# Attention and a routed expert layer in one kernel: four small moves in the order of the expert stage

## The chip, the cores and the metric

The kernel runs as one program on one core of a Trainium2 chip. The metric is device time in microseconds (us). The engines are named as in the profile: PE (TensorE), DVE (VectorE), ACT (ScalarE), POOL (GpSimd) and SP (SyncE, which issues most of the transfers). Each engine takes its instructions in the order in which the program emits them, and waits for others on semaphores.

## The reference

Inputs are `q`, `k`, `v` of 4 batches, 8 heads, 768 positions and 64 channels, a gate and the two weight matrices of each of 8 experts. First comes an attention with a window and block summaries, then a routed expert layer on its rows:

```python
mask_l = np.abs(pos[:, None] - pos[None, :]) < 16
scores_l = scale * np.matmul(q, k.transpose(0, 1, 3, 2))          # inside the window
scores_s = scale * einsum(q, k.reshape(..., 32, D).max(3)) + log(32)  # 24 block summaries
a = softmax(concat([where(mask_l, scores_l, -1e9), scores_s]))
x = a @ concat([v, block means of v])          # (4, 768, 512) after joining the heads
for each row s of a batch:
    e = argmax(x[s] @ w_gate) if local_gate(x[s]) < 0.5 or s == 0 else previous e
    h = np.maximum(x[s] @ w1[e], 0.0)           # 512 -> 1024
    out[s] = softmax(x[s] @ w_gate)[e] * (h @ w2[e])   # 1024 -> 512
```

## The kernel before

**Attention and routing.** The first third of the program is the attention, in 48 groups. Its rows go to DRAM as `x_dram`. VectorE works out each row's expert and its place in lists of rows sorted by expert (`route`, `early`, `finish`). Rows of one expert are cut into blocks of 128.

**The expert stage.** Weights are held as two parts, `hi` (rounded to a short format by an ACT cast, L1119) and `lo` (the difference, by a subtraction on DVE at L1122 or, in four pieces, on POOL at L1127). Each product is therefore three matmuls (hi by hi, hi by lo, lo by hi). `split` makes both parts of one chunk of 1024 columns; a matrix has four chunks. `SPLIT_BY` says by letters who subtracts each chunk: "VGVV" for the first matrix (chunk 1 on POOL, the others on DVE), "VVVV" for a second matrix after the first call. Raw weights come into two staging tiles `stg` by DMA from SP (`refill`, L1442), two halves of 1 MB for each matrix.

**Calls.** Blocks are served three, two or one at a time, and which calls run is decided on the chip: values are loaded into registers, and skipped calls are branched over (`tc.If`, lines 1604, 1608, 1618, 1623). With these inputs run, in order: three early pairs, `call3(0)`, `few(0)`, `call3(1)`, `few(1)`, `call3(2)` to `call3(4)`, `call2(0)`, and `call1(0)`. `few` serves up to 32 rows of an expert with unsplit weights. The experts change (new weights are split) at `call3(3)`, `call2(0)` and `call1(0)`.

**One call.** `blocks` runs the first layer (L1213 to L1215) into three rotating PSUM banks `s0`, `s1`, `s1` (printed as `bs`), each group ended by a relu on ACT (L1219) and a subtraction on DVE (L1221); then the second layer (L1165 to L1167) block by block into banks `a2` and `a` (printed `ba`). The sums of the second block are left in bank `a` ("kept"); the first block's second layer and the scaling of the kept sums are done by `left_over` at the head of the next call, where the next first-layer weights are split beside them (`hook`, `w1`). `store` scales sums into `yo` on ACT or DVE and sends them out by an indirect DMA from POOL (L1178). Second-layer weights are split by `own` beside the first layer. `late` fetches the next expert's weights into `stg` once the old ones have been read; `refill` ties such a fetch to a given matmul by a manual dependency. `single` (L1251) serves one block: its first layer goes in two runs of 12 products (`mm1(0)`, `mm1(1)`), between them four transposes (`th`), then the second layer.

**The planner.** Routing work of the last batch is woven between the matmuls of the first calls. Its steps are generators that yield a kind ("DVE", "LONG", "LONGER", "PE", ...). `flow(C_T)` is called after each short run of matmuls, moves the planner's clock on by 0.65 and emits every step that is ready by it; a DVE step adds its cost to the planner's DVE time `q` (0.1, or `C_LONG`), and a "PE" step is emitted only when the clock has reached its ready time. The four "LONGER" steps at L1051 and L1057 lead to the "PE" step of L1083, 24 matmuls that bring each slot's gate weights, and the index and scale columns of the few rows, into slot order.

**Lines touched.** `C_LONG` (L73), `left_over` (L1191), the first layer and the fetches in `blocks` (L1201), the bank of `few` (L1323), `splits` (L1457), `call2` (L1545), and the `left_over` ahead of `call1(0)` (L1619).

Of the kernel before, what the change touches and what calls it, by code (L numbers as in the profile page):

```python
# [32 lines left out]
KT, FT = DM // P, DF // P  # L33
# [8 lines left out]
AT1 = AT2 + 2 + 2 * (N2 + MORE)  # L42
SLOTS = AT1 + 2 + N1 + MORE
LANE1, LANE2 = N3 + MORE, N3 + MORE + 1
LANE3 = LANE2 + N2 + MORE
# [24 lines left out]
ON_PE = {"PE": 2, "PE late": 3}  # L70

C_T, C_PE, C_WAIT, C_DVE, C_LAT, AHEAD = 0.65, 0.8, 0.3, 0.1, 0.1, 1.5
C_LONG = {"LONG": 0.9, "LONGER": 1.7}  # L73

LOCAL_THR = -1.4e-7

# [1 line left out]
class Kernel:  # L78
# [1111 lines left out]

    def left_over(self, i, w1=None):  # L1191

        self.store(self.kept, i + 1, True)

        def hook(f):
            if w1 and f < 4:
                w1(f)

        self.store((yield from self.second_layer(0, hook)), i, True)

    def blocks(self, i, k, mid, w1=None, w2=None, between=None, refill=None, own=None):  # L1201

        nc = self.nc
        n, per = k * P, 2 if k == 2 else 1
        xT, hT = self.xT, self.hT
        xh, xl = [[xT[:, c, part, 0:k].rearrange("p h t -> p (h t)") for c in range(KT)] for part in range(2)]
        for f in range(0, FT, per):
            ps = self.bank("s")[:, 0:per * n].rearrange("p (f t) -> p f t", f=per)
            for j in range(per):
                for c in range(KT):  # L1210
                    c0 = self.w1_at(f + j, c)
                    wh, wl = [w[0][:, c0:c0 + P] for w in (self.hi, self.lo)]
                    nc.tensor.matmul(out=ps[:, j], lhsT=wh, rhs=xh[c], start=(c == 0), stop=False)  # L1213
                    nc.tensor.matmul(out=ps[:, j], lhsT=wh, rhs=xl[c], start=False, stop=False)  # L1214
                    ins = nc.tensor.matmul(out=ps[:, j], lhsT=wl, rhs=xh[c], start=False, stop=(c == KT - 1)).ins  # L1215
                    if k > 2 or c % 2:
                        yield
            h, l = hT[:, f:f + per, 0, 0:n], hT[:, f:f + per, 1, 0:n]
            nc.scalar.activation(out=h, in_=ps, func=AF.Relu)  # L1219
            self.dve(0.6, self.t + 0.5)  # L1220
            nc.vector.scalar_tensor_tensor(out=l, in0=ps, scalar=0.0, in1=h.bitcast(F32), op0=ALU.max, op1=ALU.subtract)  # L1221
            if refill and f == 0:
                refill(0, ins)
            if own and f < 4:
                own(*range(f, f + per))
            if refill and f == 4:
                refill(1, ins)
        early = w2 is not None
        halves = range(k) if early else range(k - 1, 0, -1)
        pm, last = PM0 if i == 0 else PM2 if not early and k == 2 else PM, FT * (len(halves) - 1)  # L1230
        for half in halves:

            def hook(f):
                j = FT * abs(half - halves[0]) + f
                if i > EARLY and j == pm[0]:
                    nc.gpsimd.drain()
                if j in pm:
                    mid(pm.index(j))
                if between and j == last + 4:
                    between()  # L1240
                for at, w in (PW1, w1), ([last + x for x in PW2], w2):
                    if w and j in at:
                        w(*(q for q in range(4) if at[q] == j))

            kept = not early and half == halves[-1]
            yp = yield from self.second_layer(half, hook, kept)
            if not kept:
                self.store(yp, i + half, i < EARLY or half == k - 1)
        yield
# [55 lines left out]
    def few(self, j):  # L1305


        nc, fw, xT = self.nc, self.fw, self.few_xT
        w1, w2 = self.few_w
        h = fw.tile([P, 2, P], F32, name="few_h")  # L1310
        hT = fw.tile([P, 2, 4, FEW], F32, name="few_hT")
        hp = [self.bank("s") for c in range(2)]
        for c in range(2):
            for k in range(KT):
                for q in range(4):
                    o = self.w1_at(2 * q + c, k)
                    nc.tensor.matmul(out=hp[c][32 * q:32 * q + 32, 0:P], lhsT=xT[:, k], rhs=w1[:, o:o + P], start=(k == 0), stop=(k == KT - 1))
            nc.scalar.activation(out=h[:, c], in_=hp[c][:, 0:P], func=AF.Relu)
        for c in range(2):
            m = self.bank("t")  # L1320
            nc.tensor.transpose(out=m[:, 0:P], in_=h[:, c], identity=self.ident)
            nc.vector.tensor_copy(out=hT[:, c], in_=m[:, 0:P].rearrange("p (q t) -> p q t", q=4))
        yp = self.bank("a")  # L1323
        order = [*range(0, FT, 2), *range(1, FT, 2)]
        for f in order:
            for d in range(4):
                o = f * DM + P * d
                nc.tensor.matmul(out=yp[32 * d:32 * d + 32, 0:P], lhsT=hT[:, f % 2, f // 2], rhs=w2[:, o:o + P],
                                 start=(f == order[0]), stop=(f == order[-1]))
        y = fw.tile([P, P], F32, name="few_y")  # L1330
        nc.vector.tensor_scalar(out=y, in0=yp[:, 0:P], scalar1=self.psort4[:, j:j + 1], scalar2=None, op0=ALU.mult)  # L1331
        nc.gpsimd.indirect_dma_start(out=self.out.rearrange("t (q d) -> (t q) d", q=4),
                                     out_offset=bass.IndirectOffsetOnAxis(ap=self.sidx4[:, j:j + 1], axis=0),
                                     in_=y, in_offset=None, bounds_check=4 * T_ALL - 1, oob_is_err=False)

    def run(self):
        nc, tc = self.nc, self.tc
# [110 lines left out]
        def split(w, chunks, by=None):  # L1448
            for q in chunks:
                eng = nc.vector if SPLIT_BY[by or w][q] == "V" else nc.gpsimd  # L1450
                self.split(w, q * CH, q * CH + CH, st["stage"][w][:, q * CH:q * CH + CH], eng)
# [2 lines left out]
            while "words" not in st:  # L1454
                self.small(1, True)

        def splits(w, lane):  # L1457
            new = []

            def weights(*chunks):  # L1460
                if lane is None:
                    return
                if lane == LANE1:
                    split(w, chunks)
                    if chunks[-1] == NCH - 1:
                        st["spent"].append(w)
                        refills()
                    return
                if not new:
                    have_all()  # L1470
                    new.append(reg(lane, (ENG.Activation, ENG.DVE, ENG.Pool), 1))
                with tc.If(new[0] > 0):  # L1472
                    split(w, chunks, 2 if w and lane else None)

            return weights

        def late(lane):
            r = []

            def weights(w, after):  # L1480
                have_all()
                if not r:
                    r.extend((reg(2 * LANES + lane, (ENG.SP,), 1), reg(LANES + lane, (ENG.SP,), E - 1)))
                with tc.If(r[0] > 0):
                    refill(w, r[1], after)

            return weights

        def calls(n, blocks, lane):

            def mid(half):
                if half < blocks:
                    while n < AT2 and st["next"] <= n + half:
                        self.small(1, True)
                    self.tx(n + half, half)
                    if n < AT2:
                        freed()
                    elif n + half + blocks < (AT1, SLOTS)[n >= AT1]:
                        self.gather(n + half + blocks)

            return mid, splits(0, lane), splits(1, lane)
# [9 lines left out]
        with ExitStack() as ctx:  # L1511
# [33 lines left out]
            def call2(n):  # L1545
                i = AT2 + 2 + 2 * n
                yield from self.left_over(i - 2, splits(0, LANE2 + n))
                yield from self.blocks(i, 2, calls(i + 2, 2, None)[0], None, None, None, late(LANE2 + n), splits(1, LANE2 + n))

            def emit(*what):  # L1550
                for _ in chain(*what):
                    pass
# [63 lines left out]
                self.single(i, *calls(i + 1, 1, LANE3 + n + 1), late(LANE3 + n), own)  # L1616

            with tc.If(n1 > 0) as some:
                emit(self.left_over(AT1, splits(0, LANE3)))  # L1619
                call1(0)  # L1620
                with ExitStack() as c:
                    for n in range(1, N1):
                        c.enter_context(tc.If(n1 > CALL * n))
                        call1(n)
# [93 lines left out]
```

## Time and profile before

| | us |
|---|---|
| three runs | 442.80, 446.03, 447.43 (median 446.03) |
| profiled execution, its own time | 443.36 |
| its span in the trace | 441.6 |
| PE busy | 418.5 (95%) |
| DVE busy | 233.5 (53%) |
| ACT busy | 197.6 (45%) |
| POOL busy | 175.7 (40%) |
| stage fetches (1 MB each, 16 of them), issue to landing, median | 7.8 |

The profile is of one execution. A timeline row gives the start, the length, the engine and line, what is written from what, shapes and count; in brackets, how long that engine sat idle before it and what ended the wait. Matmuls overlap, so their lengths are more than the time from one to the next. The granted TensorE clock is 1.00 of full speed (2.4 GHz) in almost all of the span.

### The profile page before, as it was taken

Reading aid. Unit: us, or ns where it says so; the run is one execution under the profiler, and the core shown is the slowest. Engines: PE = TensorE matmul, PEld = TensorE weight load, DVE = VectorE, ACT = ScalarE, POOL = GpSimd, SP = SyncE. Lnnn points to the kernel's source line nnn. Section 1 sums busy time; section 2 is a strip of 40 time slices with the busy share of each in tenths; the row PEclk is TensorE's granted clock in tenths of the full one; section 3 lists DMA queues with packets and bytes.
Section 4 is the critical chain, followed back from the end, with each engine's and each line's share of the span. In section 5 each row is a group of like instructions: output and inputs, shape, how many; then the busy total and the mean of one; then the engine's idle time right before and its main releaser. Section 6 shows DMA issues by size and latency. Waiting matters only on the chain. (4 is left out here: it accounts for less than half of the span.)

```text
span 441.6 us, 11260 instructions
## 1 busy us (share of the span) xinstructions
PE 418.5 (95%) x4228; PEld 360.7 (82%) x4228; DVE 233.5 (53%) x577; ACT 197.6 (45%) x466; POOL 175.7 (40%) x263
## 2 busy tenths in 40 slices
PE   8899989899999999999999999999999999999873
PEld 4678878678888797989987998799899899889652
DVE  5766687988775689957731122112174112247270
ACT  4968887787754217322121122122363212255451
POOL 3687585878524205845022103110350310361241
PEclk9989999999999999999999999999999999999998
DMA  8999989998260840393068802010347210309301
GB/s 315 402 364 393 388 301 357 380 406 338 71 227 19 322 197 12 98 390 123 1 242 308 345 26 77 21 49 0 95 156 276 96 49 0 94 33 382 108 24 55
DMA packets 22277, 83.24 MB, mean 189 GB/s; under 512 B 2702, under 2 KB 3344, under 8 KB 19120
## 3 DMA queue, kind: packets, MB, share of 16 engines
q1 hardware_dynamic: 17600, 67.74, 40.3%
q0 software_dynamic: 4448, 14.29, 9.4%
q8 instruction: 39, 0.64, 0.6%
q14 instruction: 46, 0.38, 0.3%
q10 hardware_dynamic: 144, 0.20, 0.1%
HBM read 69.63 MB, written 12.71 MB: 186 GB/s over the span
## 5 line engine op out<-in xcount | busy, mean ns | idle before, releaser
L1213 PE MATMUL bs<-xT,h 128*128 128x384 f32 (+1 forms) x288 | 91.4, 317 | 0.0
L1214 PE MATMUL bs<-xT,h 128*128 128x384 f32 (+1 forms) x288 | 89.8, 312 | 0.0
L1215 PE MATMUL bs<-xT,l 128*128 128x384 f32 (+1 forms) x288 | 89.7, 311 | 0.0
L1165 PE MATMUL ba<-h,hT 128*128 128x512 f32 x192 | 78.6, 410 | 2.8 <-DVE few_y L1331 1.1
L1167 PE MATMUL ba<-h,hT 128*128 128x512 f32 x192 | 75.3, 392 | 0.8 <-DVE hT L1139 0.8
L1166 PE MATMUL ba<-l,hT 128*128 128x512 f32 x192 | 75.1, 391 | 0.0
L1221 DVE SCALAR_TENSOR_TENSOR hT<-bs,hT 128x384 fp32r<-128x384 f32 (+1 forms) x56 | 33.2, 593 | 75.6 <-ACT hT L1219 61.8
L1133 POOL DMA_INDIRECT xg<-x_dram,gidx x30 | 29.7, 990 | 102.4 <-PE bt L1144 88.0
L1219 ACT ACTIVATE hT<-bs 128x384 fp32r<-128x384 f32 (+1 forms) x56 | 29.3, 523 | 85.3 <-PE bs L1215 83.4
L1213 PEld LDWEIGHTS bs<-xT,h 128*128 128x128 f32 x288 | 54.5, 189 | 0.9 <-issue 0.4
L1214 PEld LDWEIGHTS bs<-xT,h 128*128 128x128 f32 x288 | 54.5, 189 | 0.4
L1215 PEld LDWEIGHTS bs<-xT,l 128*128 128x128 f32 x288 | 54.5, 189 | 0.0
L319 ACT ACTIVATE pr<-bs,nm 128x120 f32<-128x120 f32 x192 | 51.0, 355 | 6.1 <-DVE nm L311 4.7
L1178 POOL DMA_INDIRECT out_dram<-yo,sidx x24 | 26.5, 1103 | 59.5 <-ACT yo L1174 36.1
L1122 DVE TENSOR_TENSOR l<-stg,h 128x1024 fp32r<-128x1024 f32 x26 | 35.2, 1378 | 25.1 <-ACT h L1119 24.9
L1165 PEld LDWEIGHTS ba<-h,hT 128*128 128x128 f32 x192 | 36.1, 188 | 10.6 <-issue 2.7
L1167 PEld LDWEIGHTS ba<-h,hT 128*128 128x128 f32 x192 | 36.1, 188 | 9.3 <-DVE hT L1139 1.3
L1174 ACT ACTIVATE yo<-ba,psort 128x512 f32<-128x512 f32 x24 | 16.5, 686 | 56.2 <-PE ba L1167 43.2
L1166 PEld LDWEIGHTS ba<-l,hT 128*128 128x128 f32 x192 | 36.2, 189 | 6.1
L1139 DVE TENSOR_TENSOR xT<-bt,xT 128x512 fp32r<-128x512 f32 x27 | 18.6, 691 | 40.9 <-ACT xT L1137 35.9
L1127 POOL TENSOR_TENSOR l<-stg,h 128x256 fp32r<-128x256 f32 x24 | 29.8, 1271 | 16.8 <-ACT h L1119 16.7
L1119 ACT CAST h<-stg 128x1024 fp32r<-128x1024 f32 x32 | 32.1, 1045 | 4.0 <-PE ba L1167 2.5
(265 smaller groups left out, 652.6 us busy)
## 6 DMA issues: line engine op xcount, KB each, us to landing
stg<-in_w SPq DMA_DIRECT2D x16, 1024.0 KB, 7.8
vw<-in_vW SPq DMA_DIRECT2D x16, 780.0 KB, 7.3
few_w<-in_w SPq DMA_DIRECT2D x8, 1024.0 KB, 8.5
kp<-in_kT SPq DMA_DIRECT2D x16, 384.0 KB, 6.2
q<-in_qT SPq DMA_DIRECT2D x16, 384.0 KB, 6.8
vt<-in_vT SPq DMA_DIRECT2D x16, 384.0 KB, 6.5
x_dram<-xs SPq DMA_DIRECT2D x8, 768.0 KB, 5.5
wst<-in_w SPq DMA_DIRECT2D x8, 512.0 KB, 6.8
```

Source lines behind the costliest of these rows:

```text
L319: nc.scalar.activation(out=pr[:, h, u, 0:W], in_=sp[:, h, u, :], func=AF.Exp, bias=nm[:, h, u:u + 1], scale=1.0)
L1119: self.nc.scalar.copy(out=hi, in_=src)
L1122: eng.tensor_tensor(out=lo, in0=src, in1=hi.bitcast(F32), op=ALU.subtract)
L1127: eng.tensor_tensor(out=lo[:, p], in0=src[:, p], in1=hi[:, p].bitcast(F32), op=ALU.subtract)
L1133: self.nc.gpsimd.indirect_dma_start(out=t, out_offset=None, in_=rows, in_offset=bass.IndirectOffsetOnAxis(ap=self.gidx[:, i:i + 1], axis=0))
L1165: nc.tensor.matmul(out=ps, lhsT=ah, rhs=wh, start=first, stop=False)
L1166: nc.tensor.matmul(out=ps, lhsT=ah, rhs=wl, start=False, stop=False)
L1167: self.last_mm = nc.tensor.matmul(out=ps, lhsT=al, rhs=wh, start=False, stop=last).ins
L1213: nc.tensor.matmul(out=ps[:, j], lhsT=wh, rhs=xh[c], start=(c == 0), stop=False)
L1214: nc.tensor.matmul(out=ps[:, j], lhsT=wh, rhs=xl[c], start=False, stop=False)
L1215: ins = nc.tensor.matmul(out=ps[:, j], lhsT=wl, rhs=xh[c], start=False, stop=(c == KT - 1)).ins
L1221: nc.vector.scalar_tensor_tensor(out=l, in0=ps, scalar=0.0, in1=h.bitcast(F32), op0=ALU.max, op1=ALU.subtract)
```

## The change

Four things are edited. The planner's cost of a "LONGER" step goes from 1.7 to 1.85. `left_over` scales and sends the kept sums after the four hooks that split first-layer weights, and no more ahead of them. In `blocks`, both fetches are tied to the call's very first matmul, where each was tied to the last matmul of a group, and the second matrix's fetch is emitted in group 0 where the call does not split its own second-layer weights. `few` takes its sums' bank from the rotating first-layer banks, where it took `a2`. `call2` splits its second-layer weights all at once ahead of `blocks`, and the `left_over` ahead of `call1(0)` lets DVE subtract all four first-layer chunks.

```diff
-C_LONG = {"LONG": 0.9, "LONGER": 1.7}
+C_LONG = {"LONG": 0.9, "LONGER": 1.85}
...
     def left_over(self, i, w1=None):
 
-        self.store(self.kept, i + 1, True)
-
         def hook(f):
             if w1 and f < 4:
                 w1(f)
+            if f == 4:
+                self.store(self.kept, i + 1, True)
...
+        first = None
...
-                    nc.tensor.matmul(out=ps[:, j], lhsT=wh, rhs=xh[c], start=(c == 0), stop=False)
+                    ins = nc.tensor.matmul(out=ps[:, j], lhsT=wh, rhs=xh[c], start=(c == 0), stop=False).ins
+                    first = ins if f + j + c == 0 else first
...
             if refill and f == 0:
-                refill(0, ins)
+                refill(0, first)
             if own and f < 4:
-                own(*range(f, f + per))
-            if refill and f == 4:
-                refill(1, ins)
+                own(f)
+            if refill and f == (4 if own else 0):
+                refill(1, first)
...
-        yp = self.bank("a")
+        yp = self.bank("s")
...
-        def splits(w, lane):
+        def splits(w, lane, by=None):
...
-                    split(w, chunks, 2 if w and lane else None)
+                    split(w, chunks, by or (2 if w and lane else None))
...
                 yield from self.left_over(i - 2, splits(0, LANE2 + n))
-                yield from self.blocks(i, 2, calls(i + 2, 2, None)[0], None, None, None, late(LANE2 + n), splits(1, LANE2 + n))
+                splits(1, LANE2 + n)(0, 1, 2, 3)
+                yield from self.blocks(i, 2, calls(i + 2, 2, None)[0], None, None, None, late(LANE2 + n))
...
-                emit(self.left_over(AT1, splits(0, LANE3)))
+                emit(self.left_over(AT1, splits(0, LANE3, 2)))
```

## Rows read from the trace of the kernel before

**Rows 1.** Waits of PE, whole span: us in total, times, longest.
```profile
PE bs L1166 <- POOL l L1127: 1.7, 3, 0.7
...
PE ba L1165 <- DVE few_y L1331: 1.1, 2, 0.6
...
PE ba L1167 <- DVE hT L1139: 0.8, 1, 0.8
...
PE bt L1083 <- DVE bp L1078: 0.7, 1, 0.7
```

**Rows 2.** Busy time by stretch: PE, PEld, DVE, ACT, POOL, then granted clock, DMA.
```profile
387.40:411.20 23.80, 23.61 (x152) 21.24 (x152) 13.22 (x13) 12.60 (x16) 8.87 (x8) 1.00 0.59 220
411.20:434.00 22.80, 19.30 (x84) 14.16 (x84) 11.74 (x10) 11.79 (x15) 8.65 (x7) 1.00 0.11 40
```

**Rows 3.** Timeline of PE around the planner's product at L1083.
```profile
216.28 0.33 PE L1214 MATMUL bs<-xT,h 128*128 128x384 f32 x1
216.45 0.34 PE L1215 MATMUL bs<-xT,l 128*128 128x384 f32 x1
217.47 2.28 PE L1083 MATMUL bt<-bp,A 128*128 128x202 bf16 x24 [0.68 <-DVE bp L1078]
```

**Rows 4.** Timeline of all engines at the end of `few(1)`.
```profile
281.56 1.06 PE L1328 MATMUL ba<-few_w,few_hT 128*32 128x128 f32 x32
282.69 0.35 DVE L1331 TENSOR_SCALAR few_y<-ba,psort 128x128 f32<-128x128 f32 x1 [1.62 <-PE ba L1328]
283.19 0.47 PE L1165 MATMUL ba<-h,hT 128*128 128x512 f32 x1 [0.57 <-DVE few_y L1331]
```

**Rows 5.** Timeline of all engines, last `left_over` and `single`.
```profile
412.13 0.47 PE L1165 MATMUL ba<-h,hT 128*128 128x512 f32 x1 [1.03 <-PEq L1606]
...
413.69 0.69 ACT L1174 ACTIVATE yo<-ba,psort 128x512 f32<-128x512 f32 x1 [6.08 <-DMA xg<-x_dram,gidx]
...
415.42 3.89 ACT L1119 CAST h<-stg 128x1024 fp32r<-128x1024 f32 x4 [1.04 <-issue]
...
416.50 1.23 DVE L1122 TENSOR_TENSOR l<-stg,h 128x1024 fp32r<-128x1024 f32 x1 [8.17 <-ACT h L1119]
...
417.50 4.84 POOL L1127 TENSOR_TENSOR l<-stg,h 128x256 fp32r<-128x256 f32 x4 [1.46 <-ACT h L1119]
...
417.66 0.40 PE L1165 MATMUL bs<-h,xT 128*128 128x512 f32 x1
...
418.39 6.17 DVE L1122 TENSOR_TENSOR l<-stg,h 128x1024 fp32r<-128x1024 f32 x4 [0.67 <-ACT h L1119]
...
419.80 1.98 ACT L1119 CAST h<-stg 128x1024 fp32r<-128x1024 f32 x2
...
424.35 0.60 PE L1144 MATMUL bt<-ident,hs 128*128 128x128 f32 x4
...
424.73 2.36 DVE L1122 TENSOR_TENSOR l<-stg,h 128x1024 fp32r<-128x1024 f32 x2 [0.17 <-ACT h L1119]
...
427.01 0.69 DVE L1139 TENSOR_TENSOR hT<-bt,hT 128x512 fp32r<-128x512 f32 x1
...
427.75 0.50 PE L1167 MATMUL ba<-h,hT 128*128 128x512 f32 x1 [0.83 <-DVE hT L1139]
```

**Rows 6.** Timeline of all engines in the first layer of `call2(0)`.
```profile
393.32 0.69 ACT L1174 ACTIVATE yo<-ba,psort 128x512 f32<-128x512 f32 x1
396.11 0.60 ACT L1219 ACTIVATE hT<-bs 128x512 fp32r<-128x512 f32 x1 [2.10 <-PE bs L1215]
...
401.67 0.28 PE L1213 MATMUL bs<-xT,h 128*128 128x256 f32 x1
```

**Rows 7.** Line L1127 (POOL's subtractions): durations in ns, min, median, max.
```profile
L1127 POOL TENSOR_TENSOR l<-stg,h x24: 718/822/2433, 169.7 to 420.6; 128x256 fp32r<-128x256 f32 x24
```

**Rows 8.** Timeline of SP: the last fetch of second-layer weights.
```profile
402.03 1.66 SPq L1115 DMA_DIRECT2D stg<-in_w  x2
```

**Rows 9.** DMA issues: KB each, median us from issue to landing.
```profile
stg<-in_w SPq DMA_DIRECT2D x16, 1024.0 KB, 7.8
```

More of the change, by code (lines that the diff above doesn't have):

```diff
@@ L1212, in blocks @@
                     wh, wl = [w[0][:, c0:c0 + P] for w in (self.hi, self.lo)]
-                    nc.tensor.matmul(out=ps[:, j], lhsT=wh, rhs=xh[c], start=(c == 0), stop=False)
+                    ins = nc.tensor.matmul(out=ps[:, j], lhsT=wh, rhs=xh[c], start=(c == 0), stop=False).ins
+                    first = ins if f + j + c == 0 else first
                     nc.tensor.matmul(out=ps[:, j], lhsT=wh, rhs=xl[c], start=False, stop=False)
-                    ins = nc.tensor.matmul(out=ps[:, j], lhsT=wl, rhs=xh[c], start=False, stop=(c == KT - 1)).ins
+                    nc.tensor.matmul(out=ps[:, j], lhsT=wl, rhs=xh[c], start=False, stop=(c == KT - 1))
                     if k > 2 or c % 2:
```

## Prediction

> **What bounds the kernel now.** I read three views in this order: the waits of PE over the whole span, the busy time by stretch, and the timeline at the places that the edits touch. The waits say that PE is the bound and where it still loses time that an edit could touch: differences from POOL in `single`, the few rows' scaling, one late operand of the second layer, and DVE's columns for L1083 [rows 1]. The stretches say where there is anything to win. In 387.4 to 411.2 (`call2(0)`) PE is busy 23.61 of 23.80 us, so no edit there can gain more than 0.2 us; in 411.2 to 434.0 (`left_over` and `single`) it is busy 19.30 of 22.80, both at a granted clock of 1.00, the 2.4 GHz level [rows 2]. So the sum is about places where PE stands still, and each is priced from its own timeline. An edit that moves work of another engine is worth only what PE stops waiting for.
>
> **The planner's cost.** The last product before L1083 starts at 216.45, 0.17 us after its predecessor, and L1083 at 217.47 [rows 3]. Against that pace 1.02 - 0.17 = 0.85 us are lost. Four LONGER steps lead to it, so its ready time in the planner moves by at most 4 x 0.15 = 0.60. That is under one step of 0.65, so it is emitted one step later (chance 0.60 / 0.65, about 9 in 10) or not at all later. One step here is three products, 3 x 0.174 = 0.52 us of work that PE does inside the wait. DVE's columns come when they did, so L1083 and what follows (the index of the few rows, SP's fetch of their weights) start when they did, and nothing is pushed out. Gain 0.5; bounds 0 and 0.85.
>
> **The few rows' bank.** After `few`, the next second layer writes `a2`, which DVE still reads: PE idles 0.57 us and its first product takes 0.47 instead of 0.40 [rows 4]. This happens twice, 1.1 us of idle time [rows 1]. With the sums in a first-layer bank, the last reader of `a2` is the scaling of a block that was summed before the kept one, all of `few` and a second layer of 24 products earlier. The first-layer bank is free again long before the next first layer, a whole block's second layer (24 products) later. Gain 2 x 0.65 = 1.3; bounds 0 (another wait takes its place) and 1.7 (2 x 0.85, if the restart costs nothing).
>
> **Casts first, and no POOL, in the last call.** Now ACT first scales the kept sums at 413.69, and the four casts run from 415.42 at 3.89 / 4 = 0.97 us each, after 1.04 us in which ACT waits for nothing shown. POOL subtracts chunk 1 from 417.50 to 422.34, while `single` needs chunks 0 and 1 from 417.66 on. PE restarts at 412.13 and makes 24 products by 417.66, 0.23 us each; the 18 products of `single` ahead of its transposes would end at 417.66 + 18 x 0.23 = 421.8, and the transposes stand at 424.35: 2.55 us lost [rows 5].
>
> After the change ACT can cast when it has its register: 412.13 + 1.04 = 413.2, casts until 417.1. DVE takes all four differences, the first at 414.2. The disputed price is one difference: alone it took 1.23 us and in a pair 2.36 / 2 = 1.18, beside POOL's pieces 6.17 / 4 = 1.54 [rows 5]. POOL has none left here, so I take 1.18: chunks 0 and 1 are ready at 416.6, chunks 2 and 3 at 418.9, both before PE wants them (417.7 and 420.4). The Trainium skill (SBUF — State Buffer, Who interferes with whom) says that a VectorE instruction with two SBUF inputs and a GpSimd instruction that reads SBUF shut each other out for a whole instruction; by that 1.18 holds and the sum is 4.15, and if instead 1.54 were DVE's own pace in this place the sum would be 2.3 (a rival below).
>
> Then the next thing is late, the chain that now ends in PE's wait at 427.75 [rows 5]. ACT scales the kept sums (417.1 to 417.8) and the other block's (417.9 to 418.6), casts second-layer chunks 0 and 1 from about 418.8 to 420.8 (1.98 for two), does the relu (0.60, as for this shape in [rows 6]) until 421.4, and casts chunks 2 and 3 until 423.4. DVE's last difference ends at 423.4 + 1.2 = 424.6, its difference for the transposed rows (0.69) at 425.3, and PE goes on at 425.4 where it now does at 427.75 [rows 5]. From there the order is unchanged, so the end moves with it. Gain 2.35, not 2.55, because the wait on DVE stays. Bounds: 0.5 with differences at 1.54 (the last ends at 414.2 + 8 x 1.54 = 426.5, then 0.69), and 3.5 if the 0.83 wait and its restart vanish too.
>
> **What I cost at nothing.** The same reorder in `call3(3)` and `call2(0)`: PE waits for no split there [rows 1, 2]. The kept scaling comes up to four casts (3.9 us) later; its bank is next written in that call's second layer, in `call2(0)` after the first layer whose fourth group starts at 401.67 [rows 6], and its send waits behind POOL's four pieces (4.84 us) with nothing behind it that PE needs. The fetches: SP issues the last one at 402.03 to 403.7 [rows 8], landing takes 7.8 us [rows 9], so it is in by about 411.5 and first read at 419.80 [rows 5]. Coming earlier buys nothing unless that cover of 8 us goes; SP has only these fetches queued there. If the cover went, each us late would cost one.
>
> `call2`'s second-layer split ahead of `blocks`: four casts and four differences now stand before the first relu. ACT is free at 393.32 + 0.69 = 394.0, casts at the latest from 394.8 (with the 1.04 of [rows 5] partly hidden, 0.8) to 398.7; DVE differences 395.8 to 400.5, its subtraction of group 0 (0.69) until 401.2. Group 3 wants that bank at 401.67 [rows 6]. Cost 0, but the margin is only 0.5 us; bounds 0 and 1.0 (differences at 1.54).
>
> **Sum.** 2.35 + 1.3 + 0.5 = 4.15 us. The profiled execution goes from 443.36 to 439.2 (span 441.6 to 437.45). That execution lies 2.7 under the median of the three runs, 446.03; from the median the sum gives 441.9. The four times known have a mean of 444.9, and I forecast from it: 440.8.
>
> **Rivals.**
> *A. The last call gives back its gain* (DVE, with all eight differences, becomes its bound at 1.54 each). For: PE already ends on a DVE wait there [rows 1]. Against: 1.23 and 1.18 without POOL. Gain 0.5 + 1.3 + 0.5 = 2.3: 442.6. Chance 0.18.
> *B. More than the sum*: the DVE wait at 427.75 goes as well, and L1083 loses its whole 0.85. Gain 3.5 + 1.7 + 0.85 = 6.0: 438.9. For: each bound is a row. Against: ACT's order keeps the transposed rows behind two casts. Chance 0.12.
> *C. It does not do what it says*: `a2` gives way to another wait, L1083 is not moved, and the casts wait at the head of the call for something that the kept scaling now hides. ACT idles 6.08 us ahead of that scaling, put down to a transfer [rows 5]; if the first cast needs the same release, it starts as late as now, and of 8 differences from 416.5 on at 1.18 the last ends at 425.9; with two casts between them and 0.69 PE goes on at about 427.3, a gain of 0.5. 444.4. Chance 0.08.
> *D. Slower: the bank in `call2(0)`.* ACT does relus and casts in the order emitted, so the first relu stands behind four casts, and group 3 stalls PE for every us by which DVE's first subtraction ends after 401.67. This turns the whole change into a loss from 401.67 + 4.15 = 405.8 on. POOL's pieces are the only rows that reach that far: their longest is 2.43 us [rows 7]; if each of the four differences is held up by one, they end at 395.8 + 4 x (1.18 + 2.43) = 410.2, and with 0.69 PE has lost 9.2: 444.9 - 4.15 + 9.2 = 450. Against: POOL's own chunk (4.84 in all, [rows 5]) starts with the first-layer casts, ahead of these, and a stall under 4.15 us only eats gain. Chance 0.07. The Trainium skill (PSUM — Partial Sum Buffer, Engine vs sequencer instructions) calls the queues of ScalarE, VectorE and GpSimd strict FIFO; by that rule nothing lets a relu pass the casts, which is what D needs, while the four casts on ACT's rows, run without a break, agree with it.
>
> **How the numbers follow.** The forecast as summed (gain 3.2 to 5) has 0.55, A 0.18, B 0.12, C 0.08, D 0.07. About 1% (4.4 us) is what a measurement of this kernel can tell from no change, and the sum is 0.94% of 443.36, so the forecast splits: some 45% of it beyond 1%. Faster by over 1%: 0.55 x 0.45 + 0.12 + a little for the spread of the runs = 0.40; slower by over 1%: 0.05; the rest, 0.55, within 1%. The range runs from 437.5 (B, with half of the spread of the runs below it) to 446 (A and C from the median, not from the mean); beyond it stand D and the lower end of B.
>
> **What the profile will show.** L1083's wait from 0.68 to about 0.2, with three more products ahead of it. No wait of PE on `few_y`. No row of L1127 after 411 and no PE wait on POOL; seven or more differences at about 1.2 in the last call, the first some 2 us earlier against PE's restart. The wait of L1167 on DVE still there, 0.8 to 1.2. In `call2(0)` four casts in one row ahead of the first relu, and PE without a wait at its fourth group. PE's stretch of `left_over` and `single` 2.3 us shorter. A PE wait on `bs` in `call2(0)`, a cast waiting for `stg`, or differences at 1.5 without POOL would make the prediction wrong.

## The result and the profile after

The kernel after takes 439.56 us (median of 6 runs, 438.53 to 440.91) beside 446.05 us (6 runs, 442.80 to 447.43) for the kernel before: ratio 0.9867, 95% interval 0.9829 to 0.9904, so 5.9 us faster (4.3 to 7.6). Run once more on another chip (`e12_after_again`), it has a ratio of 0.9897 (0.9855 to 0.9940). Forecast were 440.8 us and a range of 437.5 to 446.0. The profiled execution after took 439.73 us, its span is 437.9.

The end of the span moves by 3.7 us, but this understates the gain. PE's first second-layer product of the expert stage starts at 139.80 before and at 141.32 after, although no edit lies ahead of it: in the fourteen traces of this study it lies anywhere from 138.70 to 142.16. From that product to the end of the span it is 301.77 us before and 296.63 after, a gain of 5.14 (296.56 in the repeat). This stretch is what the edits act on, and it is compared below. Times are compared as ratios on one chip: the kernel before has medians from 442.99 to 446.05 us on the chips used.

Here are the waits of PE in the kernel after that answer to [rows 1].

```profile
PE ba L1167 <- DVE hT L1139: 0.8, 1, 0.8
...
PE ba L1165 <- PEq L1605: 0.6, 1, 0.6
PE ba L1165 <- PEq L1609: 0.5, 1, 0.5
```

No row is left for POOL's subtractions, for `few_y` or for L1083. The wait on `hT` has its old length.

The stretches that answer to [rows 2], of the same events (PE, PEld, DVE, ACT, POOL, granted clock, DMA):

```profile
386.74:410.52 23.78, 23.59 (x152) 21.24 (x152) 13.21 (x13) 12.23 (x16) 7.42 (x7) 1.00 0.53 203
410.52:430.40 19.88, 18.56 (x84) 14.46 (x84) 11.43 (x11) 11.67 (x15) 4.54 (x5) 1.00 0.22 66
```

`call2(0)` is as long as it was; `left_over` and `single` take 2.92 us less, of which PE stands still 2.18 less (22.80 - 19.30 = 3.50 before, 1.32 after). The rest is products that are counted as busy while the next one waits.

PE around L1083, answering to [rows 3]:

```profile
219.01 0.34 PE L1217 MATMUL bs<-xT,l 128*128 128x384 f32 x1
219.19 2.30 PE L1083 MATMUL bt<-bp,A 128*128 128x202 bf16 x24
```

It starts 0.18 us after the product ahead of it: nothing is lost. The end of `few(1)`, answering to [rows 4]:

```profile
280.72 1.95 PE L1330 MATMUL bs<-few_w,few_hT 128*32 128x128 f32 x64
...
282.60 0.50 PE L1165 MATMUL ba<-h,hT 128*128 128x512 f32 x1
...
282.74 0.35 DVE L1333 TENSOR_SCALAR few_y<-bs,psort 128x128 f32<-128x128 f32 x1 [1.62 <-PE bs L1330]
```

PE goes on before DVE has begun to read the few rows' sums. The last call, answering to [rows 5]:

```profile
410.98 0.49 PE L1165 MATMUL ba<-h,hT 128*128 128x512 f32 x1 [0.55 <-PEq L1609]
...
411.15 1.05 ACT L1119 CAST h<-stg 128x1024 fp32r<-128x1024 f32 x1 [4.20 <-DMA stg<-in_w]
...
412.23 1.23 DVE L1122 TENSOR_TENSOR l<-stg,h 128x1024 fp32r<-128x1024 f32 x1 [4.56 <-ACT h L1119]
...
413.69 2.95 ACT L1119 CAST h<-stg 128x1024 fp32r<-128x1024 f32 x3 [1.50 <-POOLq L1609]
...
414.77 3.50 DVE L1122 TENSOR_TENSOR l<-stg,h 128x1024 fp32r<-128x1024 f32 x3 [1.32 <-ACT h L1119]
...
416.55 1.25 ACT L1174 ACTIVATE yo<-ba,psort 128x512 f32<-128x512 f32 x2
...
418.77 4.74 DVE L1122 TENSOR_TENSOR l<-stg,h 128x1024 fp32r<-128x1024 f32 x4 [0.50 <-ACT h L1119]
...
423.42 0.68 DVE L1139 TENSOR_TENSOR hT<-bt,hT 128x512 fp32r<-128x512 f32 x1
...
424.16 0.50 PE L1167 MATMUL ba<-h,hT 128*128 128x512 f32 x1 [0.83 <-DVE hT L1139]
```

The first cast stands 0.17 us behind PE's restart (3.29 before), all eight differences are on DVE at 1.17 to 1.23 us, and PE's last wait is still the one for the transposed rows. From restart to last product it is 19.00 us, 21.44 before. And PE's restart itself comes 0.55 us after the last product of `call2(0)`, where it came 1.03 after: 0.48 us that no step of the prediction has.

### The profile page after: what moved, and what is told of

The parts are those of the page before. It is cut to its first block, busy times and chain, and to the rows that moved or that the text cites. A ratio compares the mean times of both kernels' runs of the same rounds, so it can differ in the third digit from the quotient of the medians.

```text
span 437.9 us, 11254 instructions
## 1 busy us (share of the span) xinstructions
PE 417.1 (95%) x4228; PEld 360.1 (82%) x4228; DVE 234.5 (54%) x578; ACT 197.7 (45%) x466; POOL 169.2 (39%) x259
## 5 line engine op out<-in xcount | busy, mean ns | idle before, releaser
L1178 POOL DMA_INDIRECT out_dram<-yo,sidx x24 | 25.0, 1042 | 63.5 <-ACT yo L1174 24.4
L276 POOL COPY vw<-vs 24x384 f32<-24x384 f32 x64 | 30.3, 514 | 6.8 <-ACT vs L271 2.9
```

What stands on the lines that cost most here:

```text
L276: nc.gpsimd.tensor_copy(out=vw[n % 3][WL:W, t:t + NW // 4, :, 0:D], in_=vs.to_broadcast([NB, NW // 4, 2, D]))
```

## The experiments

The diff holds six edits: the planner's cost, the bank of `few`, the order in `left_over`, POOL's chunk in the last call, the fetches, and the split in `call2`. The first four are tried alone on the kernel before, the last two undone in the kernel after. Each kernel has its timed ratio and, from its trace: PE's gap at the exit of `call2(0)`; how long PE's branch instruction out of it took; the time from PE's restart to the last product; and that from the first second-layer product to the end of the span.

| kernel | ratio to before (95%) | gap | branch | last call | whole stretch |
|---|---|---|---|---|---|
| before | | 1.03 | 4.61 | 21.44 | 301.77 |
| after | 0.9867 (0.9829 to 0.9904) | 0.55 | 3.55 | 19.00 | 296.63 |
| e1_planner | 0.9969 (0.9949 to 0.9989) | 1.52 | 5.09 | 20.75 | 301.02 |
| e2_few | 0.9971 (0.9946 to 0.9996) | 1.30 | 4.93 | 21.67 | 300.99 |
| e3_order | 1.0001 (0.9977 to 1.0024) | 1.27 | 4.84 | 19.64 | 300.29 |
| e4_by2 | 0.9962 (0.9936 to 0.9989) | 1.85 | 5.37 | 18.89 | 300.53 |
| e5_last | 0.9977 (0.9957 to 0.9997) | 1.37 | 4.95 | 19.06 | 299.66 |
| e6_fetch_back | 0.9897 (0.9865 to 0.9928) | 0.85 | 4.34 | 18.94 | 296.90 |
| e7_call2_back | 0.9881 (0.9850 to 0.9912) | 0.55 | 4.09 | 19.52 | 297.24 |
| e8_rows_first | 0.9843 (0.9816 to 0.9871) | 0.55 | 3.47 | 18.21 | 295.91 |
| e9_less_traffic | 0.9972 (0.9949 to 0.9996) | 0.72 | 3.89 | 19.63 | 299.85 |
| e10_more_traffic | 1.0017 (0.9984 to 1.0051) | 2.91 | 6.59 | 20.59 | 300.96 |
| e11_best | 0.9859 (0.9824 to 0.9894) | 0.56 | 3.33 | 17.66 | 295.38 |
| e12_after_again | 0.9897 (0.9855 to 0.9940) | 0.55 | 3.33 | 18.90 | 296.56 |

**e1_planner.**

```diff
-C_LONG = {"LONG": 0.9, "LONGER": 1.7}
+C_LONG = {"LONG": 0.9, "LONGER": 1.85}
```

> The kernel before with one edit: the planner's cost of a LONGER step is 1.85 instead of 1.7. Theory (the product at L1083 stands two groups of three first-layer products later, 1.04 us of work, and its columns come when they did): its wait on DVE goes from 0.68 to 0 and the place gains 0.85 us, so the time is 0.8 below the kernel before. Rival (my prediction: one group of 0.52 us): the wait is 0.2 and the gain 0.5. Rival (the columns come later by as much): no gain, a wait of 0.7 remains.

The wait of L1083 is gone:

```profile
217.37 2.30 PE L1083 MATMUL bt<-bp,A 128*128 128x202 bf16 x24
```

The stretch from the second layer ahead of L1083 to the next one falls from 26.33 to 25.50 us, 0.83, as in the kernel after. The timed gain is 1.4 us (0.5 to 2.3), which agrees. The theory of two groups holds. Why two: the prediction counted the four LONGER steps at L1051 and L1057, but `rows` (L962) yields three more of that kind on the way, so the planner's DVE time moves by 7 x 0.15 = 1.05, not by 0.60. In the emitted order L1083 stands behind 120 groups of three before, behind 121 if only the four steps or only the three cost 1.85, and behind 122 if all seven do.

**e2_few.**

```diff
-        yp = self.bank("a")
+        yp = self.bank("s")
```

> The kernel before with one edit: the few rows' second layer sums in a first-layer bank. Theory: PE's two waits on few_y (1.1 us together) go, the first product after each goes from 0.47 back to 0.40, gain 1.3 us and nothing else moves. Rival (another wait takes its place, such as the next first layer waiting for that bank): gain 0 to 0.5, with a new wait of PE in the first layer that follows.

The two stretches around `few` fall from 11.80 to 11.16 and from 11.76 to 11.13: 0.64 and 0.63, together 1.27. No new wait stands in the list of PE's. The theory holds.

**e3_order and e4_by2**, the two halves of the last call's edit. e3 moves only the scaling, e4 only takes POOL out:

```diff
-        self.store(self.kept, i + 1, True)
...
+            if f == 4:
+                self.store(self.kept, i + 1, True)
```

> The kernel before with one edit: in left_over the four first-layer casts stand ahead of the scaling of the kept sums; POOL keeps its chunk in the last call. Theory (the time was lost because the casts started late): the first cast of the last call starts 2.2 us earlier against PE's restart, POOL's chunk ends 2.2 us earlier, and the last call gains about 2.0 us. Rival (POOL's four pieces of 4.84 us and what they cost DVE beside them are the bound): the gain is at most 0.5 us, and PE still waits for POOL in the last call.

```diff
...
-                emit(self.left_over(AT1, splits(0, LANE3)))
+                emit(self.left_over(AT1, splits(0, LANE3, 2)))
```

> The kernel before with one edit: in the last left_over VectorE makes all four first-layer differences, POOL none; the scaling of the kept sums still stands ahead of the casts. Theory (late casts): casts from 415.4 as before, differences at 1.18 each, chunk 1 ready at about 418.8 where PE wants it at 417.7: PE loses 1.1 in place of 2.55 us, and with the chain behind it the gain is about 1.4 us. Rival (POOL is the whole of it): the gain is 2.3 us, as that of both edits together.

DVE, POOL and PE in e3:

```profile
417.07 1.23 DVE L1122 TENSOR_TENSOR l<-stg,h 128x1024 fp32r<-128x1024 f32 x1 [6.55 <-ACT h L1119]
...
418.07 4.88 POOL L1127 TENSOR_TENSOR l<-stg,h 128x256 fp32r<-128x256 f32 x4 [6.58 <-ACT h L1119]
...
418.97 6.20 DVE L1122 TENSOR_TENSOR l<-stg,h 128x1024 fp32r<-128x1024 f32 x4 [0.67 <-ACT h L1119]
...
423.00 0.50 PE L1166 MATMUL bs<-l,xT 128*128 128x512 f32 x1 [0.47 <-POOL l L1127]
```

ACT and DVE in e4:

```profile
417.58 3.89 ACT L1119 CAST h<-stg 128x1024 fp32r<-128x1024 f32 x4 [0.43 <-ACT yo L1174]
...
418.66 4.63 DVE L1122 TENSOR_TENSOR l<-stg,h 128x1024 fp32r<-128x1024 f32 x4 [7.41 <-PE ba L1166]
```

With POOL beside it DVE makes four differences in 6.20 us, without it in 4.63 (1.16 each). The 1.55 that the first figure gives for one is a mean of two kinds: in e3 the three that meet POOL's pieces take 1.71 to 1.76 us, and the fourth, after POOL's last piece, 1.21. POOL's first two pieces take 0.82 and 0.74, the last two, against DVE, 1.73 and 1.71.

The two edits act on one loss. It is counted from the last product of `call2(0)` to the end of the second layer (gap, last call and 0.39 for the product's own length), since the last call is shorter where PE comes back later: 22.86 before, 21.30 with the order alone, 21.13 without POOL, 20.82 with both (`e5_last`). In e1 and e2, with the last call of before, it is 22.66 and 23.36, so these are good to some tenths. By this count order and POOL are each worth 1.6 to 1.7 us alone and 2.0 together, and no one part is the whole of it. These prices are not clean, though, for the start of the first cast behind PE's restart differs even among kernels with the old order: 3.29 us before, 2.56 in e1, 3.51 in e2, 1.71 in e4, 1.46 in `e9_less_traffic` below. So e4's gain holds earlier casts that its edit does not ask for. Where the casts start alike, the last call takes 19.64 (e3) and 19.63 (e9) with POOL and 18.89 (e4) without it: some 0.7 us are POOL's, and the rest is how late the casts start.

The timed ratio of e3 shows no gain, and its interval excludes 1.6 us. One trace has to be weighed against twelve runs here; that difference stays open.

**e5_last**, both edits of `left_over` and nothing of the fetches.

> The kernel before with both edits of left_over (casts ahead of the kept scaling, all four differences on VectorE in the last call), and nothing of the fetches. Theory (the last call gains 2.5 us against PE's restart, and the exit of call2's loop is a separate matter that the fetches set): the last call gains 2.5 us, PE's gap at that exit stays at 1.0 or more as in the kernel before, and the time is 2.5 us below it. Rival (the shorter gap of the kernel after comes from these edits): the gap is 0.6 and the gain 3 us or more. Rival (both edits pay for the same loss, so one alone gives it all): no more than the 1.7 us of the better one.

The last call takes 19.06 us, 2.38 less than before, as the theory says; the gap at the exit stays above 1 us (1.37). So the shorter gap is not from these edits, and the rival falls. The timed gain is 1.0 us (0.1 to 1.9), less than the 2.1 of the stretch (301.77 - 299.66): the trace has it, the runs show half of it.

**e6_fetch_back**, the kernel after with its fetches tied as before.

```diff
-                refill(0, first)
+                refill(0, ins)
...
-            if refill and f == (4 if own else 0):
-                refill(1, first)
+            if refill and f == 4:
+                refill(1, ins)
```

> The kernel after with one edit undone: fetches wait for the last product of their group again, and second-layer weights are fetched at the fifth group in every call. Theory (the branch's code comes over the same DMA engines as the weights, so an earlier end of the fetches lets PE leave call2 on time): weights are fetched from 396 on, DMA is full until 410, PE's branch ends after its last product, its gap grows from 0.55 to 1.0 to 1.5, POOL's send no longer waits 7.6 us for the one before, and the time is 0.2 to 1.0 us above the kernel after. Rival (my prediction: coming earlier buys nothing): the gap stays at 0.55, and with POOL's send on time the kernel is 0.3 us faster than the one after. Rival (the gap is chance): it lies at 0.55 here too, or differs with no change in the DMA rows.

The gap grows to 0.85, less than the 1.0 expected, and the branch to 4.34 us. The fetches start 14.8 us ahead of the end of call2's last product, 17.0 in the kernel after and 14.6 in the one before. POOL sends on time here, at 394.90 (3.55 us after its send before), and its gathers stand at 404.30 and 405.59:

```profile
391.35 1.02 POOL L1178 DMA_INDIRECT out_dram<-yo,sidx  x1 [0.17 <-issue]
394.90 1.72 POOL L1178 DMA_INDIRECT out_dram<-yo,sidx  x1 [2.52 <-ACT h L1119]
404.30 0.98 POOL L1133 DMA_INDIRECT xg<-x_dram,gidx  x1 [7.68 <-PE bt L1144]
```

In the kernel after the second send leaves 8.37 us behind the first and the gathers start at 409.92:

```profile
393.59 1.02 POOL L1178 DMA_INDIRECT out_dram<-yo,sidx  x1 [0.17 <-issue]
401.96 1.01 POOL L1178 DMA_INDIRECT out_dram<-yo,sidx  x1 [7.35 <-ACT hT L1221]
409.92 0.98 POOL L1133 DMA_INDIRECT xg<-x_dram,gidx  x1 [6.95 <-issue]
```

The relu named there is not what a send needs, and ACT's scaling for it was done at 393.3; what differs is the 4 MB of weights that now run against the first send. In all six traces where the fetch starts with the first send (after, e7, e8, e10, e11, e12) the second leaves 8.3 to 8.7 us behind it; in e5 and e6, where the fetch starts 2 us later, 3.55. That the weights hold up the send is argued from this, and no run tests it by itself. The late POOL then holds the second cast of the last call (1.50 us, shown above). Its price is too small to read: the last call takes 18.94 us in e6, 19.00 and 18.90 in the two traces of the kernel after. The timed ratio, 0.9897, is that of the second run of the kernel after, so the runs do not resolve what the early fetch is worth; by the gap it is 0.30 us here.

**e7_call2_back**, the kernel after with call2's second-layer split between the relus again.

```diff
-                own(f)
+                own(*range(f, f + per))
...
-                splits(1, LANE2 + n)(0, 1, 2, 3)
...
+                ..., late(LANE2 + n), splits(1, LANE2 + n))
```

> The kernel after with one edit undone: call2's second-layer casts and differences stand between the relus of its first layer again, and its second-layer weights are fetched at the fifth group. Theory (the split ahead of the first layer costs PE nothing, its only effect is that the second fetch can start 3 to 5 us earlier): PE has no wait in call2's first layer in either form, the end of the DMA traffic moves by 1 us or less, and the time is within 0.5 us of the kernel after. Rival (four casts ahead of the first relu hold PE up): this kernel is 0.5 to 1 us faster.

From its first to its last second-layer product `call2(0)` takes 23.21 to 23.23 us in every trace, this one too: the split ahead of the first layer costs PE nothing. The last call is 0.5 us longer here, since its first cast starts 2.13 us behind PE's restart; why it does is not settled. The time is that of the kernel after.

**e9_less_traffic and e10_more_traffic**, to move the DMA load with the order of work left as it is. e9 is the kernel before, e10 the kernel after:

```diff
+                if w == 1 and LANE2 <= lane < LANE3:
+                    return
```

> The kernel before, with the fetch of second-layer weights in call2 left out (2 of its 4 MB; the last call then works with old second-layer weights, at the same speed). Theory (PE's branch out of call2 waits for its code, which shares the DMA engines with the weights): DMA traffic ends by 405 instead of 410, the branch takes under 4 us, and PE's gap after the last product falls from 1.0 to 1.9 us (six executions without the earlier fetch) to 0.55, as in the kernel after. Rival (the gap hangs on something else that the change touches, such as POOL's sends): it stays at 1.0 or more.

```diff
                     refill(w, r[1], after)
+                    if w == 1 and LANE2 <= lane < LANE3:
+                        refill(w, r[1], after)
```

> The kernel after, with the second-layer weights fetched twice in call2 (6 MB instead of 4). Theory: DMA traffic goes on past PE's last product of call2, the branch takes over 4.5 us, and the gap grows from 0.55 to 1.0 to 1.9 us; the second-layer weights are in by about 414 and the last call itself is no later against PE's restart. Rival (the gap hangs on the order of work in the kernel after, not on the traffic): 0.55 as in the three executions so far with the earlier fetch.

Busy time by stretch around the exit, the last two columns the DMA share and GB/s; first the kernel before, whose last product of `call2(0)` ends at 411.10:

```profile
408.00:410.00 2.00, 2.00 (x10) 1.68 (x9) 0.33 (x1) 0.00 (x0) 0.70 (x1) 1.00 0.94 340
410.00:412.00 2.00, 1.09 (x5) 0.56 (x3) 0.00 (x0) 0.00 (x0) 0.00 (x0) 1.00 0.57 170
```

Then the kernel after, where it ends at 410.44:

```profile
406.00:408.00 2.00, 2.00 (x11) 1.67 (x10) 1.23 (x2) 0.58 (x1) 0.00 (x0) 1.00 0.42 164
408.00:410.00 2.00, 2.00 (x10) 1.68 (x9) 0.00 (x0) 0.00 (x0) 0.08 (x1) 1.00 0.02 6
```

And e10, where it ends at 410.42:

```profile
408.00:410.00 2.00, 2.00 (x10) 1.68 (x9) 0.00 (x0) 0.00 (x0) 0.06 (x1) 1.00 0.97 358
410.00:412.00 2.00, 0.41 (x2) 0.00 (x0) 0.00 (x0) 0.00 (x0) 1.70 (x2) 1.00 0.96 324
```

PE's branches at that line (PEldq is PE's sequencer), durations in ns (min, median, max; the longest is the one out of `call2(0)`), in the kernel before:

```profile
L1606 PEldq COMPARE_BRANCH  x3: 73/176/4609, 387.2 to 411.7; - x3
```

in the kernel after:

```profile
L1609 PEldq COMPARE_BRANCH  x3: 73/176/3549, 386.7 to 410.6; - x3
```

and in e10:

```profile
L1611 PEldq COMPARE_BRANCH  x3: 85/176/6589, 386.7 to 413.0; - x3
```

In all fourteen traces PE's sequencer begins that branch 4.25 us ahead of the end of the last product. Where it ends ahead of the product in the kernels with the earlier fetch (after, e7, e8, e11, e12), the gap is 0.55 or 0.56 us; where it ends behind it, the gap is longer by what it is late and up to 0.2 us more. Where the weights are in at least 2 us ahead of the product, the branch takes 3.3 to 4.1 us, where they come in its last 1 us, 4.3 to 5.4, with 2 MB more 6.59. e10 has the order of the kernel after and the longest gap of all, so order is not the cause, and the rival falls. e9 has the order of the kernel before and 3.89 us; its gap is 0.72, not the 0.55 expected, and its wait is put down to DVE's exit. That the code comes over the same DMA engines shows in the instruction packets among the weights' in this stretch (DMA queues of the kernel before, 404.0 to 411.1):

```profile
q1 hardware_dynamic: 308, 2.14, 72.4%
...
q14 instruction: 5, 0.04, 1.8%
q8 instruction: 1, 0.02, 1.0%
```

The traces also show which packet it is. In all fourteen one instruction packet of 16 KB stands in queue 8 during this branch, and the branch ends 1.31 to 1.36 us after that packet has ended. The packet takes 0.99 to 1.22 us everywhere; what differs is how long after the branch's own start it begins: 1.0 us in e8, e11 and e12, 1.25 in the kernel after, 1.6 in e9, 1.8 in e7, 2.19 in the kernel before (1.9 to 2.9 in all with the late fetch) and 4.17 in e10. So the branch waits for its code, and the code comes late when the weights still run.

The Trainium skill (DMA: Bandwidth & Descriptors, Queues, rings and completion order) calls row 14 runtime-internal and lists refill among its uses, which agrees with the name of that row here; the packet that ends PE's branch stands in row 8, so in this the measurement decides. The Trainium skill's figure for a compare-and-branch (Advanced Engine Details and Errata, Control Flow Timing: about 108 ns) is of the size of the short ones here (73 to 176 ns), not of those that wait for code: the measurement decides.

e9 shows one thing more. With neither edit of `left_over`, its last call takes 19.63 us, 1.81 less than in the kernel before:

```profile
411.05 0.47 PE L1165 MATMUL ba<-h,hT 128*128 128x512 f32 x1 [0.72 <-DVEq L1608]
411.64 0.69 ACT L1174 ACTIVATE yo<-ba,psort 128x512 f32<-128x512 f32 x1 [4.79 <-DMA xg<-x_dram,gidx]
412.51 3.89 ACT L1119 CAST h<-stg 128x1024 fp32r<-128x1024 f32 x4 [0.18 <-ACT yo L1174]
```

ACT scales 0.59 us behind PE's restart and casts 0.18 us after that; before it was 1.56 and 1.04 [rows 5]. The count of e3 and e4 gives 20.74 here, as little as with both edits. So part of the last call's loss before was ACT coming late, not the order alone, and it can shrink with less traffic too. One trace shows it (the timed gain of e9 is 1.2 us, 0.2 to 2.3), and what ACT waited for there is open.

**e8_rows_first and e11_best.** Both start from the kernel after and go for the wait on `hT`. e8 puts `own(2, 3)` behind the first transposed rows; e11 divides it:

```diff
-        if own:
-            own(2, 3)
         mm1(1, (0, 1))
         hT = [self.th(hs[0], 0), None]
+        if own:
+            own(2)
         mm1(1, (2, 3))
+        if own:
+            own(3)
```

> The kernel after with one more edit: in single the casts and differences of second-layer chunks 2 and 3 stand behind those of the first transposed rows. Theory (PE's last wait of 0.83 us comes from the order on ACT and VectorE): the wait of L1167 on hT goes to 0.1 or less, chunks 2 and 3 are ready before the product that needs them, and the time is 0.7 us below the kernel after. Rival (my prediction's bound: another wait takes its place): the second transposed rows or chunk 2 come late, and the gain is 0.2 or less.

> The kernel after with one more edit: in single, chunk 2 of the second-layer weights is cast behind the first transposed rows, and chunk 3 behind the second relu. Theory (what is left of the last call's loss when both chunks go behind the first rows is the second relu waiting behind the cast of chunk 3, 0.5 us at the second transposes): no wait of PE on hT and none on hs over 0.1 us, the stretch from the first product of single to the last falls from 13.43 (after) and 12.65 (both chunks behind the rows) to 12.2, and the time is 1.2 us below the kernel after. Rival (chunk 3 comes too late for the products that need it): a new wait of PE at the fifth to eighth pair of second-layer products, and 12.6 or more.

In e8 the wait on `hT` is gone and a smaller one takes its place: the second relu stands behind two casts. Its stretch is 0.7 us under that of the kernel after, as forecast.

```profile
422.38 2.00 ACT L1119 CAST h<-stg 128x1024 fp32r<-128x1024 f32 x2
...
424.28 0.60 ACT L1265 ACTIVATE hs<-bs 128x512 f32<-128x512 f32 x1
...
424.93 0.66 PE L1144 MATMUL bt<-ident,hs 128*128 128x128 f32 x4 [0.34 <-ACT hs L1265]
```

In e11 cast, relu and cast alternate, and PE has no wait in the last call:

```profile
420.67 1.05 ACT L1119 CAST h<-stg 128x1024 fp32r<-128x1024 f32 x1
...
421.62 0.60 ACT L1265 ACTIVATE hs<-bs 128x512 f32<-128x512 f32 x1
...
422.11 1.05 ACT L1119 CAST h<-stg 128x1024 fp32r<-128x1024 f32 x1
...
422.73 0.60 PE L1144 MATMUL bt<-ident,hs 128*128 128x128 f32 x4
```

From the first product of `single` to the last it is 13.43 us in the kernel after, 12.65 in e8 and 12.11 in e11 (12.2 forecast). e11 takes 437.10 us beside 442.99 for the kernel before on its chip, 1.41% less (1.06% to 1.76%). Its stretch is 1.2 us under that of the kernel after; the timed intervals of the two overlap and do not separate them.

**e12_after_again**, unchanged.

> The kernel after once more, unchanged, beside the kernel before on another chip. Theory (the places in the traces hold all of it, 5.1 us from PE's first second-layer product to the end, and what the first comparison showed above that, 5.9, is the chance of the stage ahead of it): ratio near 1 - 5.1 / 444 = 0.9885, the stretch from that product to the end 296.6 within 0.5, PE's gap at call2's exit 0.55 and its wait on hT 0.8. Rival (the change also gains in the stage ahead, which no edit touches): ratio of 0.986 or less with the same stretch.

0.9897 and 296.56 us: the stretch holds the gain, and the part of the first 5.9 us that lies above 5.1 is within the spread.

## Why the prediction was right, step by step

| step | forecast | trace |
|---|---|---|
| L1083 | 0.5 | 0.83 |
| few rows' bank, twice | 1.3 | 1.27 |
| restart to last product | 2.35 | 2.44 |
| exit of `call2(0)` | 0 | 0.48 |
| exit ahead of `call2(0)` | 0 | 0.11 |
| reorder, split, all else | 0 | 0.01 |
| sum | 4.15 | 5.14 |

**The last call** went as told: casts right after PE's restart, differences at 1.17 to 1.23, the same wait on DVE at the end, with its 0.83 us. The edits do it without the earlier fetch as well (e5, 2.38 us). PE goes on 13.18 us after its restart (forecast 425.4 - 412.13 = 13.27). One part went otherwise: the first cast came 0.17 us after the restart instead of 1.1, but the second waited 1.50 us for POOL, so the kept scaling began 5.57 us after the restart, where 4.97 were forecast. The reason given is right in part: the casts were late not only because the scaling stood ahead of them, since in e9 they start 1.46 us after the restart with the scaling still ahead. That 2.35 was met so closely is in part luck, for the old last call takes 20.75 to 21.67 us in the three traces with neither of its edits and the full traffic. The price of 1.54 for a difference beside POOL is a mean of three at 1.70 to 1.74 and one alone at 1.21; it entered only the bounds and rival A.

**The few rows' bank** was right to 0.03 us.

**L1083** was mis-sized: "it is emitted one step later" is the line that failed. It counted four of the seven steps whose cost rose; two steps gave the whole 0.85.

**The fetches**: "coming earlier buys nothing" is the step that was wrong. It asked only when the weights are read, and not what else shares the DMA engines. The last packet of the weights now ends 2.3 us ahead of the last product of `call2(0)` instead of 0.4, and PE's way out is 0.48 us shorter in this pair. Against the six traces of the kernel before and of e1 to e5 (gaps 1.03 to 1.85, mean 1.39) it is 0.84 shorter, against e6, which undoes only the fetches, 0.30. So the step had the mechanism wrong, and what it is worth is known only to lie between 0.3 and 0.8.

**The sends**: "with nothing behind it that PE needs" held for PE, but the send now meets the weights' traffic, the next one waits, and POOL reaches the last call 3.5 us later (gathers at 409.92, 406.45 before). In the last call that costs nothing that can be read (19.00 and 18.90 beside 18.94 in e6), though ACT waits 1.50 us.

**The four casts in `call2(0)`** stand in one row, and the fourth group has no wait, as forecast:

```profile
393.39 3.89 ACT L1119 CAST h<-stg 128x1024 fp32r<-128x1024 f32 x4
...
397.19 0.59 ACT L1221 ACTIVATE hT<-bs 128x512 fp32r<-128x512 f32 x1
```

The Trainium skill's strict FIFO for these queues (PSUM — Partial Sum Buffer, Engine vs sequencer instructions) agrees: the relu follows the casts. The Trainium skill's rule on two SBUF inputs (SBUF — State Buffer, Who interferes with whom), an exclusive lock between DVE and GpSimd, agrees with e3: 1.71 to 1.76 us for a difference that meets POOL's pieces, 1.21 for one that does not.

**The rivals.** A fell (differences at 1.17 to 1.23), C fell, D fell (`call2(0)` did not get longer). B, more than the sum, was nearer than its chance of 0.12 says: 5.1 lies between the forecast's 4.15 and B's 6.0, and the L1083 half of B came true. The split of chances, 0.55 on "within 1%" and 0.40 on faster, leant the wrong way by the one microsecond of the missed steps. That 440.8 came within 1.3 us of 439.56 owes something to luck as well: it was taken from a mean of 444.9, and from the 446.05 that stood beside it in the end the same sum gives 441.9.

## What to carry to other kernels

That nobody waits for a transfer's data does not mean that its time is of no matter: ask what else uses the DMA engines in the time that it leaves empty or fills, the code behind a branch and other queues' sends among them. When a loss is priced from one trace, look at the same place in other traces: the same code lost 1 us more or less here. When a planner's cost changes, count every step of that kind on the way to the product, not only the nearest. And compare the stretch that the edits act on, from one event to another, when a stage ahead of it varies by more than the gain.

## What the runs showed of the hardware

PE's branch over the calls that do not run takes 3.33 us where the weights' traffic ends 1.8 us into it (e12) and 6.59 where it lasts throughout (e10), while the two others at that line take 0.07 to 0.19. It ends 1.31 to 1.36 us after one 16 KB instruction packet, which with more traffic comes up to 4.17 us after the branch's start instead of 1.0.

In e10 PE stood still for 2.91 us at that exit. Soon after it went on, its clock fell (busy time by stretch; the granted clock is third from the end):

```profile
411.50:414.70 3.20, 1.37 (x6) 1.17 (x7) 0.00 (x0) 0.00 (x0) 0.69 (x1) 0.99 0.93 348
414.70:418.00 3.30, 3.30 (x10) 2.53 (x9) 0.60 (x1) 1.69 (x2) 0.00 (x0) 0.50 0.11 40
418.00:420.00 2.00, 2.00 (x10) 1.66 (x9) 2.00 (x3) 2.00 (x3) 0.00 (x0) 0.99 0.02 8
```

For 3.3 us the clock is 0.50, the 1.2 GHz level, and products follow each other at 0.43 us instead of 0.23. `left_over` takes 7.18 us instead of 5.57, so the stop cost 1.6 us more than itself. After 1.85 us of standing still (e4) `left_over` took 5.56, without such a loss.

A difference of 1024 columns on DVE takes 1.21 us alone; against POOL's pieces both take longer, DVE 1.71 to 1.76 and POOL 1.71 to 1.73 for what is 0.74 to 0.82 before (e3).
